# Two buffers for a group of W', the fifth transpose in another bank, and one chunk's stores on another queue

## The chip, the cores and the metric

The kernel runs on one core of a Trainium2 chip. The core's engines take their instructions in order, each from its own list, and wait for each other through semaphores: TensorE (PE in the profile; PEld is its loading of weights), VectorE (DVE), ScalarE (ACT), GpSimd (POOL) and SyncE (SP). SyncE only issues DMAs here; ScalarE issues some as well. The metric is the device time of one execution in microseconds (us), the median over several.

## The reference, cut to what matters

The output is a mix of two branches, weighted per token by a gate `g`. Branch A is a Fourier transform along the hidden and the sequence dimension, real part only. Branch B picks experts per head by two small score tables and sums their outputs.

```python
def reference(x, dft_seq_re, dft_seq_im, dft_hid_re, dft_hid_im, w_q, k1, k2, u, v, gate_w):
    g = sigmoid((x * gate_w).sum(-1, keepdims=True))
    # branch A
    a = einsum("bsd,ed->bse", x, dft_hid_re)
    b = einsum("bsd,ed->bse", x, dft_hid_im)
    y = einsum("ts,bse->bte", dft_seq_re, a) - einsum("ts,bse->bte", dft_seq_im, b)
    # branch B, per token and head: q = x w_q in two halves of 128
    s1, s2 = q1 @ k1.T, q2 @ k2.T              # 16 scores each
    # the best 2 of each, the best 2 of their 4 sums, softmax of those: gates; their pairs: experts
    out = sum over heads and picks of gates * gelu(x . u[expert]) * v[expert]
    return g * y + (1 - g) * out
```

Shapes: 2048 tokens, width 640, 32 heads, 16 x 16 = 256 experts, float32.

## The kernel before

All matrix products are done in float32 by a split: each operand is cut into a high and a low half (ScalarE writes the high half, line 122; GpSimd or VectorE subtracts it to get the low half, line 123), and three matmuls, high x high, high x low and low x high (`mm3`, lines 127 to 129), make one product.

The program is written in the order in which it is issued. It has 128 **pieces** of branch A (`seq_piece`): two matrices (real, imaginary), 4 chunks of 512 tokens, 16 pieces each. A piece is 15 matmuls of 128x512 into banks 0 to 4 and splits the matrix block of the piece three further on (`WS`, a ring of four). A block is loaded five pieces ahead (`wf`, line 159). A table `then`, filled by `at(n, ...)`, hangs other work behind piece n. At the end of a chunk ScalarE copies the five banks into the stage `ST` (line 220), VectorE multiplies the five parts with the gate (line 192, `gate_piece`), and the parts are stored to DRAM as `pd`, the partial sums P (line 201, `store_piece`).

In the first pieces the scores' weights are prepared: W', which is `w_q` multiplied with the keys. It is made in 8 groups G of 128 columns. For a group, a burst of 32 small matmuls (`w_part`, line 320) fills banks 5 and 6 in turn (`ps_s`), ScalarE copies both halves into the tile `wp` (line 325), and five transposes (`w_transposes`, line 331) turn the 640 rows around; ScalarE and VectorE write the result as a high and a low half into `WU` (lines 333 and 334). Four transposes are issued in one call, ahead of the next group's burst, the fifth a piece later in a second call. Both calls write into bank 7 (`ps_t`). The burst of group G is hung behind piece 6 + 3G; only behind piece 28 do two calls stand next to each other: the fifth transpose of group 6 and then the four of group 7. `wp` has one buffer. A copy into it therefore waits until the fifth transpose of the group before has been done, though that stands a piece later in TensorE's order.

From piece 31 on the scores, the picks and the experts' sums are put among the pieces. After the last piece comes a **last part** of 70 **steps** (`step`): the sequence product's second stage, written as sums of blocks, with operands loaded back from DRAM (`ra`). Step m uses the split operand m (in the tiles `WP` for m mod 6 below 2, else in `WS`), which was split five steps earlier (`split_step`), and 6 or 9 matmuls. The last chunk's stores (q = 7) are hung behind step 1 of it. `split_v` (a split of `v`, whose high half's and low half's parts ScalarE negates in line 736) and `split_z` (the operands `zo`, whose products VectorE makes in lines 851 and 852) fall into the same stretch.

DMAs take turns on eight semaphores, in the order in which the program issues them, whichever engine issues. A DMA waits until the one before it on its semaphore has landed; in the lists of instructions these are DMAHW0 to DMAHW7.

Of the kernel before, what the change touches and what calls it, by code (L numbers as in the profile page):

```python
# [8 lines left out]
F32 = mybir.dt.float32  # L9
# [7 lines left out]
P = 128  # L17
S = 2048
D = 640
# [8 lines left out]
NC = S // TC  # L28
# [62 lines left out]
def gated_mix_kernel(ctx: ExitStack, tc: tile.TileContext, xT, xn, dreT, dimT, wsre, wsim, wq, kT, uT, vv, gw, out):  # L91
    nc = tc.nc
# [9 lines left out]
    def rotate(what, n):  # L102
        turn[what] = (turn.get(what, -1) + 1) % n
        return turn[what]

    def bank(n, shape=(P, TC), dt=F32):
        return psum.tile(list(shape), dt, name=f"b{n}", tag=f"b{n}")

    def ps_s(shape=(P, TC)):
        return bank(5 + rotate("pss", 2), shape)  # L110

    def ps_t(shape, dt=F32):
        return bank(7, shape, dt)
# [17 lines left out]
    pd = {(w, c): dram.tile([KD, P, TC], F32, name=f"pd{w}{c}", tag=f"pd{w}{c}") for w in range(2) for c in range(NC)}  # L131
# [49 lines left out]
    grow, staged, P22 = {}, {}, {}  # L181
# [14 lines left out]
    def store_piece(q):  # L196
        w, c = divmod(q, NC)
        if q == NC + 1:
            P22.update((d, staged[q, d]) for d in range(KD))
        for d in range(KD):  # L200
            nc.scalar.dma_start(pd[w, c][d], staged.pop((q, d)))

    def seq_piece(n):
        w, c, s = pieces[n]
# [18 lines left out]
    for q in range(2 * NC):  # L223
        n = NT * (q + 1)
        at(n + (2 if q == 0 else -2 if q > 1 else -1), load_row, q)
        at(n + (7 if q == 0 else 0), gate_piece, q)
        at(n + (8 if q == 0 else 1), store_piece, q)
# [3 lines left out]
    p1 = p1_stack.enter_context(tc.tile_pool(name="p1", bufs=1, reuse_waits="tile"))  # L231
# [43 lines left out]
    t = ps_t([P, 512])  # L275
# [28 lines left out]
    wqs, wps, wp = {}, {}, {}  # L304
# [8 lines left out]
    def w_part(m):  # L313
        G, r, n = m // 4, m // 2 % 2, m % 2
        if r == 0:
            wps[G, n] = ps_s()
        ps = wps[G, n]
        w = wqs.pop(m)
        for j in range(4):
            nc.tensor.matmul(ps[32 * j:32 * j + 32, :HALF], kp[:, 8 * G // H, r, :], w[:, j], start=(r == 0),  # L320
                             stop=(r == 1))
        if r == 1:
            if n == 0:
                wp[G] = p1.tile([P, D], F32, name="wp", bufs=1)
            nc.scalar.activation(wp[G][:, n * HALF:(n + 1) * HALF], wps.pop((G, n))[:, :HALF], AF.Copy)

    def w_transposes(G, k0, k1):
        f = wp[G]
        t = ps_t([P, 4, P])
        for k in range(k0, k1):  # L330
            nc.tensor.transpose(t[:, k - k0, :], f[:, k * P:(k + 1) * P], identf)  # L331
        h = WH[:, k0:k1, P * G:P * (G + 1)]
        nc.scalar.activation(h, t[:, :k1 - k0], AF.Copy)  # L333
        nc.vector.tensor_sub(WL[:, k0:k1, P * G:P * (G + 1)], t[:, :k1 - k0], h.bitcast(F32))  # L334
# [35 lines left out]
    for G in range(NG + 1):  # L370
        b = 6 + 3 * G - 2 * (G == NG)
        if G:
            at(b, w_transposes, G - 1, 0, 4)
        if G < NG:
            for m in range(4 * G, 4 * G + 4):
                at(b, w_part, m)
            for i, m in enumerate(range(4 * G + WQB, 4 * G + WQB + 4)):
                at(b + i // 2, load_wq, m)
        if G:
            at(b + 1, w_transposes, G - 1, 4, KD)  # L380
# [702 lines left out]
```

## Time and profile before

| | |
|---|---|
| median of 3 runs | 782.41 us (782.23 to 783.89) |
| the profiled execution | 782.4 us |
| its span in the profile | 780.6 us |
| mean granted clock of TensorE | 0.998 of full speed |
| matmuls of branch A, W', scores, experts and last part | 4116 |
| DMA traffic | 130.32 MB, mean 167 GB/s |

The profile is one execution. Times are counted from the start of its span, which is a little shorter than the execution's own time, since what lies around the first and last instruction is not in it. A row of the timeline has the start, the duration, the engine, the line of the kernel, the operation, what is written and read, a count, and in brackets how long the engine had been idle and what ended that. ACTq and SPq rows are DMA issues of ScalarE and SyncE. Busy TensorE means that matmuls are in flight; a matmul's own duration of 0.39 us is longer than the 0.23 us after which the next one starts, since they overlap.

### The profile page before, as it was taken

The page shows a single profiled execution, that of the slowest core. Times are in us where ns is not written, and L with a number is a line of the kernel's source. Part 1 is how long each engine was busy: PE and PEld are TensorE (multiplying, and loading weights), DVE is VectorE, ACT ScalarE, POOL GpSimd, SP SyncE. Part 2 cuts the span into 40 slices and gives each one's busy share as a digit, 9 for nine tenths or more (in the row PEclk, how much of TensorE's full clock was granted, in tenths as well). Part 3 has the DMA queues.
Part 4 walks back from the last instruction along what each step waited for, and adds up shares of the span by engine and source line. Part 5 has one row for each costly group of instructions (what it writes and reads, how often), then busy time and mean ns, then how long its engine had stood idle before and what let it go on. Part 6 is the DMA issues. An engine that isn't in the chain of part 4 may idle for free.

```text
span 780.6 us, 11020 instructions
## 1 busy us (share of the span) xinstructions
PE 769.4 (99%) x4116; PEld 624.5 (80%) x4116; DVE 564.5 (72%) x660; ACT 274.0 (35%) x445; POOL 333.7 (43%) x233
## 2 busy tenths in 40 slices
PE   9999998999999999999999999999999999999997
PEld 6777776888888888888888888888888877888886
DVE  5742032279799799999989889698989857728561
ACT  5435223322233531533532461311324533424350
POOL 5432324323432324234156574343447463558270
PEclk9999999999999999999999999999999999999999
DMA  9887894512212241221353443558945767477321
GB/s 339 330 300 192 346 337 148 178 51 88 69 53 71 69 159 57 65 86 54 97 169 123 152 147 94 162 185 291 300 174 174 237 241 243 127 253 242 122 81 68
DMA packets 75509, 130.32 MB, mean 167 GB/s; under 512 B 17088, under 2 KB 24128, under 8 KB 75200
## 3 DMA queue, kind: packets, MB, share of 16 engines
q1 hardware_dynamic: 62704, 112.18, 43.4%
q10 hardware_dynamic: 12752, 17.45, 6.2%
q8 instruction: 32, 0.52, 0.3%
q14 instruction: 21, 0.17, 0.1%
HBM read 102.84 MB, written 25.17 MB: 164 GB/s over the span
## 4 chain that ended last, share of the span: by engine, by line
PE 88%; DVE 4%; issue 3%; POOL 3%; DMA 1%; ACT 0%; SPq 0%; DVEq 0%; POOLq 0%; ACTq 0%
PE b L127 28%; PE b L128 28%; PE b L129 28%; PE b L320 2%; POOL WS L123 1%; PE b L625 1%; POOL WP L123 1%; DMA wf<-in_wsre 1%; PE b L331 1%; DVE tf L710 1%; DVE tf L713 1%; DVE ts L123 0%; DVE tmp L611 0%; DVE tf L711 0%; DVE hot L604 0%
## 5 line engine op out<-in xcount | busy, mean ns | idle before, releaser
L123 POOL TENSOR_TENSOR WS<-wf,WS 128x512 fp32r<-128x512 f32 x127 | 191.5, 1513 | 263.3 <-ACT WS L122 263.3
L127 PE MATMUL b<-WS,X 128*128 128x512 f32 x635 | 250.9, 395 | 0.0
L128 PE MATMUL b<-WS,X 128*128 128x512 f32 x635 | 247.8, 390 | 0.2 <-POOL WS L123 0.2
L129 PE MATMUL b<-WS,X 128*128 128x512 f32 x635 | 247.6, 390 | 0.0
L127 PEld LDWEIGHTS b<-WS,X 128*128 128x128 f32 x635 | 119.4, 188 | 29.2 <-issue 4.1
L129 PEld LDWEIGHTS b<-WS,X 128*128 128x128 f32 x635 | 119.5, 188 | 25.2
L128 PEld LDWEIGHTS b<-WS,X 128*128 128x128 f32 x635 | 119.5, 188 | 24.8 <-POOL WS L123 0.8
L122 ACT ACTIVATE WS<-wf 128x512 fp32r<-128x512 f32 x128 | 80.7, 631 | 136.8 <-PE b L129 83.3
L123 POOL TENSOR_TENSOR xl<-xf,xh 128x640 fp32r<-128x640 f32 x16 | 27.1, 1694 | 84.6 <-ACT xh L122 84.6
L127 PE MATMUL b<-WU,xh 128*128 128x512 f32 x160 | 62.3, 390 | 0.0
L128 PE MATMUL b<-WU,xh 128*128 128x512 f32 x160 | 62.3, 390 | 0.0
L129 PE MATMUL b<-WU,xl 128*128 128x512 f32 x160 | 62.2, 389 | 0.0
L439 DVE TENSOR_REDUCE mm<-sc 128x64 f32<-128x1024 f32 x32 | 38.9, 1217 | 27.0 <-ACT sc L425 26.4
L123 POOL TENSOR_TENSOR WS<-ra,WS 128x512 fp32r<-128x512 f32 x32 | 44.9, 1423 | 31.2 <-ACT WS L122 22.4
L425 ACT ACTIVATE sc<-b 128x512 f32<-128x512 f32 x32 | 19.8, 619 | 108.0 <-PE b L129 102.3
L441 DVE TENSOR_TENSOR eq<-sc,mm 128x1024 f16<-128x1024 f32 x32 | 49.9, 1559 | 1.1
L611 DVE TENSOR_TENSOR tmp<-b,mask 128x512 f32<-128x512 f32 x32 | 22.0, 689 | 34.8 <-PE b L625 33.8
L334 DVE TENSOR_TENSOR WU<-b,WU 128x512 fp32r<-128x512 f32 (+1 forms) x16 | 7.8, 490 | 50.8 <-ACT WU L333 50.8
L123 POOL TENSOR_TENSOR WP<-ra,WP 128x512 fp32r<-128x512 f32 x18 | 27.7, 1546 | 33.5 <-ACT WP L122 33.4
L192 DVE SCALAR_TENSOR_TENSOR ST<-ST,grow 128x512 f32<-128x512 f32 x40 | 37.0, 987 | 4.1 <-ACT ST L220 4.1
L445 DVE TENSOR_REDUCE rr<-eq 128x64 f16<-128x1024 f16 x32 | 39.0, 1219 | 1.0
L122 ACT ACTIVATE WS<-ra 128x512 fp32r<-128x512 f32 x46 | 28.3, 630 | 28.0 <-PE b L129 16.7
(156 smaller groups left out, 1257.0 us busy)
## 6 DMA issues: line engine op xcount, KB each, us to landing
wq<-in_wq SPq DMA_DIRECT2D x32, 640.0 KB, 6.8
wf<-in_wsre SPq DMA_DIRECT2D x64, 256.0 KB, 4.8
wf<-in_wsim SPq DMA_DIRECT2D x64, 256.0 KB, 3.6
ra<-pd SPq DMA_DIRECT2D x50, 256.0 KB, 4.1
pd<-ST ACTq DMA_DIRECT2D x40, 256.0 KB, 3.1
xr<-in_xn SPq DMA_DIRECT2D x16, 320.0 KB, 5.8
xf<-in_xT SPq DMA_DIRECT2D x16, 320.0 KB, 3.3
ra<-pqs SPq DMA_DIRECT2D x20, 256.0 KB, 5.1
```

Of the source, the lines that this page charges most:

```text
L122: nc.scalar.activation(h, f, AF.Copy)
L123: eng.tensor_sub(l, f, h.bitcast(F32))
L127: nc.tensor.matmul(o, wh, ah, start=first, stop=False, skip_group_check=more)
L128: nc.tensor.matmul(o, wh, al, start=False, stop=False, skip_group_check=more)
L129: nc.tensor.matmul(o, wl, ah, start=False, stop=last, skip_group_check=more)
L192: nc.vector.scalar_tensor_tensor(f, f, -1.0 if w else 1.0, g, op0=OP.mult, op1=OP.mult)
L320: nc.tensor.matmul(ps[32 * j:32 * j + 32, :HALF], kp[:, 8 * G // H, r, :], w[:, j], start=(r == 0), stop=(r == 1))
L425: nc.scalar.activation(scs[i].rearrange("p h e -> p (h e)")[:, c], ps, AF.Copy)
L439: nc.vector.tensor_reduce(m, sc, op=OP.max, axis=AX.X)
L441: nc.vector.tensor_tensor(eq, sc, m[:, :, None].to_broadcast([P, HH, E]), op=OP.is_equal)
L445: nc.vector.tensor_reduce(r, eq, op=OP.max, axis=AX.X)
L611: nc.vector.tensor_tensor(tmp, t.rearrange("p m (e t) -> p (m e) t", t=4), mask4[:, None, :].to_broadcast([P, 8 * E, 4]), op=OP.mult)
```

## The change

Three edits: `wp` gets two buffers; the second call of the transposes (the fifth, `k0` = 4) takes its bank from `ps_s` (banks 5 and 6 in turn) instead of bank 7; and the five stores of the last chunk are issued by SyncE instead of ScalarE.

```diff
@@ store_piece
+        eng = nc.sync if q == 2 * NC - 1 else nc.scalar
         for d in range(KD):
-            nc.scalar.dma_start(pd[w, c][d], staged.pop((q, d)))
+            eng.dma_start(pd[w, c][d], staged.pop((q, d)))
@@ w_part
             if n == 0:
-                wp[G] = p1.tile([P, D], F32, name="wp", bufs=1)
+                wp[G] = p1.tile([P, D], F32, name="wp", bufs=2)
@@ w_transposes
         f = wp[G]
-        t = ps_t([P, 4, P])
+        t = ps_s((P, 4, P)) if k0 else ps_t([P, 4, P])
```

One line is added ahead of line 201, so lines behind it have a number higher by one in the changed kernel.

The first place is TensorE behind piece 28. The number behind a name is that of the tile; `b7_1140` is a tile in bank 7, `wp_999` and `wp_1106` are groups 6 and 7. Before:

```order
L129 MATMUL b4_699<-WS_88,X_442 128x512
L331 MATMUL b7_1140<-identf_148,wp_999 128x128 [waits DVE_49]
L331 MATMUL b7_1144<-identf_148,wp_1106 128x128 [waits DVE_49]
L331 MATMUL b7_1144<-identf_148,wp_1106 128x128
L331 MATMUL b7_1144<-identf_148,wp_1106 128x128 [waits Activation_49]
L331 MATMUL b7_1144<-identf_148,wp_1106 128x128
```

And now:

```order
L129 MATMUL b4_699<-WS_88,X_442 128x512
L332 MATMUL b5_1140<-identf_148,wp_999 128x128 [waits Activation_49]
L332 MATMUL b7_1144<-identf_148,wp_1106 128x128 [waits DVE_49]
L332 MATMUL b7_1144<-identf_148,wp_1106 128x128
L332 MATMUL b7_1144<-identf_148,wp_1106 128x128 [waits Activation_49]
L332 MATMUL b7_1144<-identf_148,wp_1106 128x128
```

The order is the same. The fifth transpose has moved to bank 5 and waits for ScalarE, which empties that bank of group 7's burst. The first of the four still waits for VectorE, but for the four of group 6, which were the last in bank 7.

The second place is ScalarE in the last part, at the last chunk's stores (`pd13` is that chunk of P). Before:

```order
L736 ACTIVATE ts_4959<-vxl_5322 128x256 [waits DVE_49]
L122 ACTIVATE WP_5185<-ra_5208 128x512 [waits DMAHW0_49,PE_49,Pool_49]
L201 DMA pd13_76<-ST_68 128x512 [waits DMAHW6_49]
L201 DMA pd13_76<-ST_68 128x512 [waits DMAHW0_49]
L201 DMA pd13_76<-ST_68 128x512 [waits DMAHW2_49]
L201 DMA pd13_76<-ST_68 128x512 [waits DMAHW4_49]
L201 DMA pd13_76<-ST_68 128x512 [waits DMAHW6_49]
L122 ACTIVATE WP_5185<-ra_5210 128x512 [waits DMAHW3_49,PE_49,Pool_49]
L122 ACTIVATE WS_88<-ra_5235 128x512 [waits DMAHW5_49,PE_49,Pool_49]
```

And now:

```order
L737 ACTIVATE ts_4959<-vxl_5322 128x256 [waits DVE_49]
L122 ACTIVATE WP_5185<-ra_5208 128x512 [waits DMAHW0_49,PE_49,Pool_49]
L122 ACTIVATE WP_5185<-ra_5210 128x512 [waits DMAHW3_49,PE_49,Pool_49]
L122 ACTIVATE WS_88<-ra_5235 128x512 [waits DMAHW5_49,PE_49,Pool_49]
L122 ACTIVATE zo_5374<-ra_5286 128x512 [waits DVE_49]
```

The splits of steps 6, 7 and 8 (`ra_5208`, `ra_5210`, `ra_5235`) now follow each other; before, the five stores stood between the first and the second.

The third place is SyncE's list in the same stretch, with the loads of the next operands (`pqs1`, `pqs2`). Now:

```order
L770 DMA ra_5327<-pqs1_77 128x512 [waits DMAHW2_49,PE_49]
L770 DMA ra_5327<-pqs1_77 128x512 [waits DMAHW3_49]
L202 DMA pd13_76<-ST_68 128x512 [waits DMAHW4_49,DVE_49]
L202 DMA pd13_76<-ST_68 128x512 [waits DMAHW5_49,DVE_49]
L202 DMA pd13_76<-ST_68 128x512 [waits DMAHW6_49,DVE_49]
L202 DMA pd13_76<-ST_68 128x512 [waits DMAHW7_49,DVE_49]
L202 DMA pd13_76<-ST_68 128x512 [waits DMAHW0_49,DVE_49]
L770 DMA ra_5346<-pqs1_77 128x512 [waits DMAHW1_49,DVE_49]
L770 DMA ra_5346<-pqs1_77 128x512 [waits DMAHW2_49]
L770 DMA ra_5091<-pqs2_78 128x512 [waits DMAHW3_49,Pool_49]
```

Before, the loads stand in the same order without the stores between them. The stores wait for VectorE's product with the gate, each for its own part, and the loads behind them wait for other semaphores than before.

## The prediction

> **What bounds the kernel now.** I read the busy times first, then who waited for whom on TensorE, then the granted clock in the stretches where it waited. Of the profile's first part, one line matters:
>
> ```profile
> PE 769.4 (99%) x4116; PEld 624.5 (80%) x4116; DVE 564.5 (72%) x660; ACT 274.0 (35%) x445; POOL 333.7 (43%) x233
> ```
>
> TensorE (PE) works for 769.4 of the 780.6 us of the span, so only about 11 us can be won without taking matmuls away. No edit here takes any away. The waits of PE over the whole span (us in total, times, longest) say where those 11 us lie, apart from the last stores:
>
> ```profile
> PE b L331 <- DVE WU L334: 3.5, 1, 3.5
> PE b L277 <- DVE warm L274: 1.2, 1, 1.2
> PE b L128 <- POOL WP L123: 0.8, 1, 0.8
> PE b L128 <- POOL WS L123: 0.8, 2, 0.6
> PE b L213 <- ACT WS L122: 0.4, 1, 0.4
> ```
>
> Two of them belong to the start. The other three places are one transpose (line 331) that waited 3.5 us for VectorE, and two matmuls of the last part that waited for GpSimd's low halves. I take the places in turn.
>
> **The transposes: what goes.** PE's rows (start, duration) around the long wait, with undisturbed neighbours, show how matmuls and transposes follow each other:
>
> ```profile
> 122.66 0.60 PE L331 MATMUL b<-identf,wp 128*128 128x128 f32 x4
> 123.19 2.36 PE L320 MATMUL b<-wq,kp 128*32 128x320 f32 x32
> ...
> 129.02 0.27 PE L331 MATMUL b<-identf,wp 128*128 128x128 f32 x1
> 132.77 1.11 PE L331 MATMUL b<-identf,wp 128*128 128x128 f32 x4 [3.48 <-DVE WU L334]
> 133.53 0.78 PE L127 MATMUL b<-WS,X 128*128 128x512 f32 x1
> ...
> 135.80 0.39 PE L129 MATMUL b<-WS,X 128*128 128x512 f32 x1
> ...
> 137.87 0.39 PE L129 MATMUL b<-WS,X 128*128 128x512 f32 x1
> ...
> 138.43 0.39 PE L128 MATMUL b<-WS,X 128*128 128x512 f32 x1
> ```
>
> At 129.02 the fifth transpose of group 6 goes into bank 7, and the four of group 7 stand right behind it in the same bank. They start at 132.77, when the fifth has been copied out. Only here do the two calls meet without a chunk's piece between them. The copying out is late because of what ScalarE and VectorE do from 129 on:
>
> ```profile
> 129.38 0.77 ACT L325 ACTIVATE wp<-b 128x320 f32<-128x320 f32 x2 [5.49 <-PE b L331]
> ...
> 132.11 0.27 ACT L333 ACTIVATE WU<-b 128x128 fp32r<-128x128 f32 x1
> ...
> 132.42 0.29 DVE L334 TENSOR_TENSOR WU<-b,WU 128x128 fp32r<-128x128 f32 x1 [1.51 <-ACT WU L333]
> ```
>
> ScalarE stood still for 5.49 us: its copies into `wp` for group 7 wait until the fifth transpose has read the only buffer. Behind them in its order come three splits, and only then the fifth's copy. With two buffers these copies need only the burst of line 320, which ends at 123.19 + 2.36 = 125.55, and are done by about 126.4. The three splits then run before 129, and the fifth's copy follows its transpose at once.
>
> The second edit makes the rest certain: the fifth transpose goes into a bank of the bursts, which ScalarE has emptied by 126.4. The four of group 7 use bank 7, last read by VectorE's subtraction for group 6, a whole piece earlier. So both calls find their banks free, and I cost their waits at nothing.
>
> The price of the wait is more than 3.48 us, as the granted clock (PEclk, the column behind the busy times) shows. These rows give, for a stretch, its length and the engines' busy time:
>
> ```profile
> 129.00:132.70 3.70, 0.29 (x2) 0.00 (x0) 0.71 (x2) 3.00 (x7) 1.55 (x2) 0.96 0.00 0
> 132.70:136.00 3.30, 3.23 (x10) 2.75 (x11) 1.19 (x3) 1.42 (x3) 3.30 (x3) 0.53 0.23 47
> ```
>
> After the wait PE ran at 0.53 of its clock until about 135.8, so four transposes took 1.11 us instead of 0.60. I therefore measure the gain at the sixth matmul behind them, where the pace is whole again, at 135.80. Undisturbed matmuls follow each other by 0.23 us (135.80 to 137.87 in nine). A fifth transpose between two of them adds 0.10 (138.43 less 137.87 less 2 x 0.23). Four transposes take 0.53 until the next starts (123.19 less 122.66). Without the wait the four start at 129.12, the first matmul at 129.65, and the sixth at 129.65 + 5 x 0.23 = 130.80. The gain is 135.80 less 130.80 = **5.0 us**: 3.65 of waiting and 1.35 of slow clock.
>
> In the other groups ScalarE waits for the fifth transpose in the same way, but that costs PE nothing now, since its waits above have no row for it; the end of those waits gains nothing. A group's second burst bank is now also read by VectorE for the fifth transpose, but ten microseconds before the next burst; I cost that at nothing too.
>
> **What is late next there.** The scalar and vector work shifts earlier with PE. One thing is tied to something else: SyncE's loads, which stand behind a load into `xf` whose buffer GpSimd reads.
>
> ```profile
> 131.15 3.03 POOL L123 TENSOR_TENSOR xl<-xf,xh 128x640 fp32r<-128x640 f32 x2 [8.13 <-ACT xh L122]
> 134.22 0.80 SPq L352 DMA_DIRECT2D xf<-in_xT  x2
> ```
>
> GpSimd waited 8.13 us for ScalarE's split, which is one of the three behind the `wp` copies. With those at 126.4 instead of 130.15 it starts some 3.8 us sooner, and so does the load. Against PE's 5.0 the pieces of `wf` behind it are 1.2 us later than now, and PE waits for none of them now. Later, a uniform shift needs an engine that follows PE and is not itself behind. Waits of VectorE from 145 to 620 us:
>
> ```profile
> DVE mm L439 <- ACT sc L425: 26.4, 5, 12.6
> DVE tmp L611 <- PE b L625: 20.2, 10, 3.4
> ```
>
> It stood idle for PE or for PE's results 15 times; so it follows, and the 5.0 us arrive whole.
>
> **The stores: what goes.** PE around its two late waits:
>
> ```profile
> 635.00 0.39 PE L129 MATMUL b<-WP,DD 128*128 128x512 f32 x1
> 635.46 0.50 PE L127 MATMUL b<-WP,DD 128*128 128x512 f32 x1
> 636.81 0.50 PE L128 MATMUL b<-WP,DD 128*128 128x512 f32 x1 [0.85 <-POOL WP L123]
> 637.15 0.39 PE L129 MATMUL b<-WP,DD 128*128 128x512 f32 x1
> ...
> 640.82 0.39 PE L127 MATMUL b<-WS,DD 128*128 128x512 f32 x1
> 641.82 0.50 PE L128 MATMUL b<-WS,DD 128*128 128x512 f32 x1 [0.61 <-POOL WS L123]
> ```
>
> These are steps 7 and 9. At its pace the third row of step 7 would stand at 635.00 + 3 x 0.23 = 635.69; it stands at 637.15, so the place costs 1.46. In step 9 the second matmul would start at 641.05 instead of 641.82, and restarting costs 0.11 (0.34 behind the wait instead of 0.23): 0.88. Both together are **2.34 us**, the most the third edit can give. Its cause is on ScalarE and GpSimd:
>
> ```profile
> 630.93 3.72 ACTq L201 DMA_DIRECT2D pd<-ST  x4
> 634.78 0.63 ACT L122 ACTIVATE WP<-ra 128x512 fp32r<-128x512 f32 x1 [3.39 <-DMA pd<-ST]
> ...
> 631.47 1.76 POOL L123 TENSOR_TENSOR WP<-ra,WP 128x512 fp32r<-128x512 f32 x1 [4.21 <-ACT WP L122]
> 635.49 1.27 POOL L123 TENSOR_TENSOR WP<-ra,WP 128x512 fp32r<-128x512 f32 x1 [2.25 <-ACT WP L122]
> 636.72 1.29 POOL L123 TENSOR_TENSOR WS<-ra,WS 128x512 fp32r<-128x512 f32 x1
> 637.96 2.57 POOL L123 TENSOR_TENSOR zo<-ra,zo 128x512 fp32r<-128x512 f32 x2
> ```
>
> Four stores held ScalarE for 3.72 us, so the split of step 7 came late and GpSimd stood still for 2.25. Without them ScalarE splits step 7 right behind step 6, and GpSimd goes on at 633.23 without a gap. How fast it goes on is the unknown. From 632.00 to 634.51 VectorE still has two products of the weights `z`, and the two engines delay each other:
>
> ```profile
> 623.83 3.43 POOL L123 TENSOR_TENSOR WS<-ra,WS 128x512 fp32r<-128x512 f32 x2
> ...
> 632.00 1.78 DVE L851 TENSOR_TENSOR ra<-ra 128x512 f32<-128x512 f32 x1
> 633.82 0.69 DVE L852 TENSOR_TENSOR ra<-ra 128x512 f32<-128x512 f32 x1
> ```
>
> GpSimd's subtraction took 1.72 beside busy VectorE (3.43 for two), 1.27 alone; the product took 1.78 against 0.69. Undelayed, GpSimd ends step 7 at 634.50, step 8 at 635.75, both `zo` at 638.25 and step 9 at 639.55. PE now wants step 9's low half at 641.05 less 1.46 = 639.59, so the whole 2.34 is won. With steps 7 and 8 at 1.72 each, step 7 ends at 634.95 (PE wants it at 635.46 to 635.69), step 8 at 636.67, `zo` at 639.2 and step 9 at 640.5: PE waits 0.9 and pays 0.11 for the restart, and 1.3 us are won. I take **1.3**, since both products are still to come when GpSimd would go on; 0 and 2.34 are the ends.
>
> [...]
>
> **What the stores do on SyncE.** Five issues and their waits now stand ahead of 18 loads. They wait for VectorE's products with the gate, done by 628.94. The first load behind them waited 8.8 us anyway:
>
> ```profile
> SPq L769 <- DVE ra L848: 8.8, 1, 8.8
> ...
> 639.98 1.15 ACT L122 ACTIVATE WP<-ra 128x512 fp32r<-128x512 f32 x2
> ```
>
> It was let go near 630.45, after VectorE's split of `v`, which comes behind those products. So the stores issue in a hole of SyncE's and delay no load; they leave earlier than now. ScalarE wants that load only at 639.98.
>
> **The sum.** The profiled execution took 782.4 us, its span 780.6 and 1.8 around it; the median of the runs is 782.41, so no correction is needed. 782.4 - 5.0 - 1.3 = **776.1 us**.
>
> **Rivals.** *The stores win nothing*: GpSimd stays late in the last part, because VectorE's products hold it or the loads come later on SyncE. For it: GpSimd is back to back from 635.49 to step 9. Against it: the 2.25 us gap in it goes. Time 782.4 - 5.0 = 777.4, give or take 0.3.
>
> *Part of the long wait stays*: the four transposes of group 7 wait for `wp`, whose copies now come just ahead of them, or PE meets a later split. For it: GpSimd and ScalarE still have three splits between. Against it: 126.4 against 129.12 leaves 2.7 us. With between 0.3 and 3.5 us left at PE the time is 777.7 to 780.8. [...]
>
> *The first two edits do not do what they say*: bank 7 stays the meeting point. Then only the stores count, 782.4 - 1.3 = 781.1, no measurable change. The rows of the two calls, with different banks, speak against it.
>
> *Slower, through SyncE*: the stores hold the queue and the loads behind them starve the last part. A load takes SyncE about 5 us to land, so from 630.45 it is there at 635.5, and ScalarE wants it at 639.98: 4.5 us are free. To eat the 6.3 us won elsewhere the stores would have to hold SyncE for about 11 us past 630.45, though what they wait for is done at 628.94. Time above 784 from there on.
>
> **How the numbers follow.** Forecast, 774.8 to 777.1: 0.66. Stores win nothing, 777.1 to 777.7: 0.17. Part of the wait stays, 777.7 to 780.8: 0.10. No effect, within 0.2% (780.8 to 784.0, about what a measurement of this kernel can tell from no change): 0.04. Slower: 0.03. The low end is the whole 7.3 us, 775.1, with 0.3 of spread; the high end takes in the second case: 774.8 to 777.7 holds 0.83. Faster by over 0.2%: 0.66 + 0.17 + 0.10 = 0.93.
>
> **What would show it.** Right: no wait of line 332 on VectorE, ScalarE's `wp` copies near 126, and a clock of 1.00 from 129 to 136. In the last part, ScalarE's split of step 7 right behind that of step 6, GpSimd without a gap from 631 less 5, and one wait of PE under 1 us at step 9. Wrong: a new wait of PE between 129 and 150, a slow clock without a wait, or SyncE's loads of the last part later against PE than now.

## The result and the profile after

The changed kernel takes 775.41 us (median of 6 runs, 774.75 to 775.75) beside 783.15 us (median of 6, 782.23 to 784.94): a ratio of 0.9899, 95% interval 0.9885 to 0.9912. The profiled executions are 775.65 and 782.4 us, 6.75 us apart. The forecast was 776.1, with 774.8 to 777.7 around it.

TensorE in the first part of the page, then the waits of PE over the whole span (us in total, times, longest):

```profile
PE 767.0 (99%) x4116; PEld 623.2 (81%) x4116; DVE 565.7 (73%) x660; ACT 275.2 (36%) x445; POOL 332.6 (43%) x233
```

```profile
PE b L128 <- POOL WS L123: 1.3, 2, 0.8
PE b L278 <- DVE warm L275: 1.2, 1, 1.2
PE b L214 <- ACT WS L122: 0.2, 1, 0.2
```

The transposes' row is gone, and so is that of step 7 (`WP`). What is left on GpSimd is one wait of the start and one of 0.75 us at step 9. PE at the place of the long wait (start, duration):

```profile
129.18 0.71 PE L332 MATMUL b<-identf,wp 128*128 128x128 f32 x5
129.64 0.48 PE L127 MATMUL b<-WS,X 128*128 128x512 f32 x1
...
130.88 0.40 PE L129 MATMUL b<-WS,X 128*128 128x512 f32 x1
```

The five transposes now run as one group, and the sixth matmul behind them starts at 130.88 instead of 135.80. The same stretches as before, with the granted clock behind the busy times, show it at full speed:

```profile
129.00:132.70 3.70, 3.70 (x20) 3.08 (x19) 1.59 (x3) 1.70 (x4) 3.70 (x3) 1.00 0.37 107
132.70:136.00 3.30, 3.30 (x16) 2.69 (x15) 0.29 (x1) 0.80 (x2) 1.96 (x3) 1.00 1.00 349
```

ScalarE and GpSimd there, and SyncE's load that stood behind GpSimd:

```profile
125.24 0.98 ACT L326 ACTIVATE wp<-b 128x320 f32<-128x320 f32 x2 [1.19 <-PE b L321]
...
129.48 0.28 ACT L334 ACTIVATE WU<-b 128x128 fp32r<-128x128 f32 x1 [1.19 <-PE b L332]
...
127.22 3.10 POOL L123 TENSOR_TENSOR xl<-xf,xh 128x640 fp32r<-128x640 f32 x2 [5.39 <-ACT xh L122]
...
130.34 0.80 SPq L353 DMA_DIRECT2D xf<-in_xT  x2
```

The copies into `wp` are released by the burst (line 321) and no longer by the fifth transpose; the fifth's own copy comes 0.3 us behind it. The last part, on ScalarE, GpSimd, PE and SyncE:

```profile
625.84 1.14 ACT L122 ACTIVATE WP<-ra 128x512 fp32r<-128x512 f32 x2
...
626.53 3.48 POOL L123 TENSOR_TENSOR WP<-ra,WP 128x512 fp32r<-128x512 f32 x2 [4.21 <-ACT WP L122]
629.97 1.75 POOL L123 TENSOR_TENSOR WS<-ra,WS 128x512 fp32r<-128x512 f32 x1
...
635.51 0.50 PE L128 MATMUL b<-WS,DD 128*128 128x512 f32 x1 [0.75 <-POOL WS L123]
...
619.50 4.92 SPq L202 DMA_DIRECT2D pd<-ST  x5
625.50 11.55 SPq L770 DMA_DIRECT2D ra<-pqs  x18
```

Steps 6 and 7 are split back to back on both engines. GpSimd takes 1.74 us for each and 1.75 for step 8. SyncE issues the five stores as VectorE's products come and is done a microsecond before the 18 loads may start.

Where the 6.7 us of the span come from can be read by comparing the same instructions in both traces. Up to the fifth transpose (129.02 before, 129.18 now) the changed kernel is 0.16 us behind, as its start was. At the sixth matmul it is 4.92 ahead, so the place gave about 5.1. The bursts of the experts' sums stand 4.95 us ahead from the first (437.24 before, 432.29 now) to the one at 619.02 (614.07 now), and 6.35 ahead behind step 9 (644.58 and 638.23): the last part gave 1.40. The remaining 0.4 or so lie behind the last matmul, where the last stores land, and no edit touches them.

### The profile page after: what moved, and what is told of

Its sections match the earlier page's. It is cut to its first block, busy times and chain, and to the rows that moved or that the text cites. A ratio compares the mean times of both kernels' runs of the same rounds, so it can differ in the third digit from the quotient of the medians.

```text
span 773.9 us, 11025 instructions
## 1 busy us (share of the span) xinstructions
PE 767.0 (99%) x4116; PEld 623.2 (81%) x4116; DVE 565.7 (73%) x660; ACT 275.2 (36%) x445; POOL 332.6 (43%) x233
## 4 chain that ended last, share of the span: by engine, by line
PE 89%; DVE 4%; issue 3%; POOL 2%; DMA 1%; SPq 0%; DVEq 0%; ACT 0%; POOLq 0%
PE b L127 29%; PE b L128 28%; PE b L129 28%; PE b L321 2%; POOL WS L123 1%; PE b L626 1%; DMA wf<-in_wsre 1%; DMA ra<-pqs 1%; DVE tf L711 1%; PE b L332 1%; POOL WP L123 1%; DVE tf L714 1%; DVE ts L123 0%; DVE tmp L612 0%; DVE tf L712 0%
## 5 line engine op out<-in xcount | busy, mean ns | idle before, releaser
L192 DVE SCALAR_TENSOR_TENSOR ST<-ST,grow 128x512 f32<-128x512 f32 x40 | 35.1, 938 | 4.1 <-ACT ST L221 4.1
```

The costliest lines, as they stand in the source:

```text
L192: nc.vector.scalar_tensor_tensor(f, f, -1.0 if w else 1.0, g, op0=OP.mult, op1=OP.mult)
```

## The experiments

The executions of the kernel before lie between 780.7 and 785.1 us in all that follows. Each comparison has the kernel before on the same chip; the first four kernels share one set of it (median 782.36).

**One edit alone: two buffers.**

```diff
-                wp[G] = p1.tile([P, D], F32, name="wp", bufs=1)
+                wp[G] = p1.tile([P, D], F32, name="wp", bufs=2)
```

> Only the second buffer of wp; the fifth transpose stays in bank 7. Theory: the long wait was a late copying out, not the shared bank alone. ScalarE reaches the fifth's copy (0.28 us) at once and VectorE (0.29 us) follows, so the four of group 7 still wait, but only about 0.9 us, and the granted clock from 132 to 136 us stays 1.00. Time 4.1 us below the kernel before. Rival (bank 7 is the whole cause): the wait stays near 3.5 us and nothing is won. Rival (any wait here halves the clock): 0.9 us of wait and 1.35 of slow clock stay, 2.8 us won.

Measured: 778.02 us (777.76 to 778.67), ratio 0.9947 (0.9934 to 0.9960), 4.3 us below. The row of PE's wait and the granted clock behind it:

```profile
PE b L331 <- DVE WU L334: 0.7, 1, 0.7
```

```profile
132.70:136.00 3.30, 3.30 (x16) 2.68 (x15) 0.29 (x1) 0.80 (x2) 1.69 (x2) 1.00 0.99 341
```

The bank is still shared, and the wait is 0.7 us long instead of 3.5: its length was the late copying out. Both rivals fall: the wait did not stay, and the clock behind the short one is whole.

**One buffer, but no shared bank.** The second edit cannot stand alone: with one buffer the fifth transpose would wait for a burst bank whose copy waits for the fifth transpose. So the four transposes of the last group were moved instead.

```diff
-        t = ps_t([P, 4, P])
+        t = ps_s((P, 4, P)) if k0 == 0 and G == NG - 1 else ps_t([P, 4, P])
```

> One buffer of wp; the four transposes of group 7 go into a burst bank, so that they do not meet the fifth of group 6 in bank 7. Theory: they now wait for the copies into wp, which still wait for the fifth (ScalarE idle about 34 us in 7 waits, as before): about 1.1 us of wait at PE, no slow clock, 3.9 us below the kernel before. Rival (the shared bank is the whole cause): no wait of PE, 5.1 us won.

Measured: 778.16 us (777.57 to 778.39), ratio 0.9946 (0.9933 to 0.9959), 4.2 us below, with a wait of 0.6 us where the theory had 1.1; the rival, no wait, falls. What ended PE's wait has changed, and ScalarE's old wait is still there (tile `wp`: what its engine waited for):

```profile
PE b L331 <- ACT wp L325: 0.6, 1, 0.6
```

```profile
  PE b L331: 34.1, 7
```

So the 3.5 us needed both: the one buffer that made ScalarE late and the bank that made PE wait for ScalarE's lateness. Either remedy alone, the second buffer or another bank for these transposes, takes out most of it, and the two edits together (777.36 us, below) 0.7 to 0.8 us more than one.

**The stores alone.**

```diff
+        eng = nc.sync if q == 2 * NC - 1 else nc.scalar
         for d in range(KD):
-            nc.scalar.dma_start(pd[w, c][d], staged.pop((q, d)))
+            eng.dma_start(pd[w, c][d], staged.pop((q, d)))
```

> Only the last chunk's stores on SyncE. Theory: the 3.5 us wait and the slow clock stay; step 7 waits no more, step 9 about 0.75 us; 1.4 us below the kernel before. Rival (the last part's gain needs the earlier edits, or the stores are not its cause): no difference, 0 +- 0.3 us.

Measured: 780.85 us (778.84 to 782.30, 12 runs), ratio 0.9978 (0.9967 to 0.9988), 1.5 us below. More of its executions than of the kernel before kept a whole clock (a mean of 0.999 or more: 5 of 12 against 2 of 17), so compare like with like: 1.3 us between the medians of those with a lowered clock (781.05 and 782.39), 1.8 of those without (779.10 and 780.87). Step 7 has no wait left. Its profiled execution, the fastest of the twelve, brought a surprise: the long wait is there, and the clock behind it is not lowered.

```profile
PE b L332 <- DVE WU L335: 3.5, 1, 3.5
```

```profile
132.70:136.00 3.30, 3.30 (x17) 2.76 (x16) 1.65 (x2) 1.42 (x3) 3.30 (x3) 1.00 0.35 111
```

**The first two edits without the stores.**

> Both edits of the transposes, the stores left on ScalarE. Theory: no wait of PE on a transpose, clock 1.00, and the waits of 0.85 and 0.61 us at steps 7 and 9 as before: 5.1 us below the kernel before. Rival (part of the 5.1 is lost later without the third edit): under 4 us won, with larger waits in the last part.

Measured: 777.36 us (776.74 to 778.05), ratio 0.9937 (0.9924 to 0.9950), 5.0 us below, with PE's wait of 0.9 us at step 7 still there. 5.0 and 1.5 make 6.5; the whole change, run again (next), is 7.3 below its own set of the kernel before, whose executions scatter. The parts add up within that scatter; the intervals of the ratios allow it.

**The whole change again, and three variants of the last part** (one chip; kernel before 782.9).

> The changed kernel again, beside the three next ones on one chip. Theory: the first two edits gave 5.0 us and the third 1.5 us apart, and they do not meet; so 6.5 to 7.0 us below the kernel before, every execution within about 1 us, none with a mean clock below 0.999.

Measured: 775.58 us (775.21 to 775.65), ratio 0.9908 (0.9895 to 0.9922). No mean clock was below 0.999.

Next the stores were left on ScalarE but hung later; they then write what the stage holds after step 4's copies, so that chunk of P has other values.

```diff
-    at(n + (8 if q == 0 else 1), store_piece, q)
+    at(n + (8 if q == 0 else 8 if q == 2 * NC - 1 else 1), store_piece, q)
```

> Both edits of the transposes; the last chunk's stores stay on ScalarE but are hung behind step 8 instead of step 1. Theory: what the third edit won is ScalarE's place in the list, not the queue of SyncE; step 7's split runs at once, and the time is that of the changed kernel within 0.4 us, if the stage's buffers, which the copies of steps 4 and 9 write, are not the next wait. Rival (those copies now wait behind nothing, but the copy after step 4 needs the stored part and stands ahead of the stores): ScalarE's copy order changes and a new wait takes 1 us or more.

Measured: 777.69 us (776.78 to 779.26), ratio 0.9938 (0.9926 to 0.9951): no better than with the stores left where they were. Half of the theory is in the rows: step 7's split follows step 6's at once, from 625.60 on, and PE has no wait at step 7. Its condition fails. The late stores hold ScalarE for 4.47 us, and then its copy into the stage's fifth buffer (line 959) waits 4.00 us for a store to land, since the store still has to read that buffer; PE waits for the copy:

```profile
634.19 4.47 ACTq L201 DMA_DIRECT2D pd<-ST  x4
638.78 0.63 ACT L122 ACTIVATE WS<-ra 128x512 fp32r<-128x512 f32 x1 [4.24 <-DMA pd<-ST]
```

```profile
643.42 0.60 ACT L959 ACTIVATE ST<-b 128x512 f32<-128x512 f32 x1 [4.00 <-DMA pd<-ST]
...
644.07 0.50 PE L127 MATMUL b<-WS,DD 128*128 128x512 f32 x1 [0.66 <-ACT ST L959]
```

That wait and its restart cost about 0.9 us; the profiled execution is 1.2 above the whole change's and the median 2.1, and the rest is not explained. So the stores cost something at both places tried on ScalarE, but for different reasons, and this run does not settle whether the engine that issues or the place in its list is what counts. An earlier place on ScalarE is untested. In the kernel before it stands idle just ahead of the stores' place, for longer than the 4.92 us in which SyncE issues all five in the changed kernel:

```profile
630.45 0.42 ACT L736 ACTIVATE ts<-vxl 128x256 fp32r<-128x256 f32 x1 [5.60 <-DVE vxl L123]
```

Then VectorE's products for the first `zo` were left out.

```diff
-            nc.vector.tensor_tensor(a, a, f, op=OP.mult)
-            nc.vector.tensor_tensor(a, a, g, op=OP.mult)
+            if b or n:
+                nc.vector.tensor_tensor(a, a, f, op=OP.mult)
+                nc.vector.tensor_tensor(a, a, g, op=OP.mult)
```

> The changed kernel without VectorE's four products of the first operands zo (they hold the activations alone, so the experts' part of one chunk is wrong). Theory: the remaining wait at step 9 (0.75 us, 0.86 with the restart) comes from VectorE and GpSimd delaying each other; GpSimd's subtractions of steps 7 and 8 take 1.27 instead of 1.75 us, and PE has no wait there: 0.9 us below the changed kernel. Rival (GpSimd simply has too much in a row, seven subtractions): step 9 still waits 0.3 us or more.

Measured: 774.6 us (774.22 to 774.77), ratio 0.9896 (0.9882 to 0.9909), 1.0 below the whole change. GpSimd's rows for steps 6, 7 and 8:

```profile
626.61 2.55 POOL L123 TENSOR_TENSOR WP<-ra,WP 128x512 fp32r<-128x512 f32 x2 [4.21 <-ACT WP L122]
629.12 1.29 POOL L123 TENSOR_TENSOR WS<-ra,WS 128x512 fp32r<-128x512 f32 x1
```

Two take 2.55 us instead of 3.48, the third 1.29 instead of 1.75, and PE has no wait in the last part. The wait at step 9 came from VectorE and GpSimd hindering each other.

Last, a version that should be faster: VectorE, idle from 630.6, subtracts step 9's low half.

```diff
-            split(raw[key], *sp[m], nc.vector if what in ("s2", "s3") else nc.gpsimd)
+            split(raw[key], *sp[m], nc.vector if what in ("s2", "s3") or m == 9 else nc.gpsimd)
```

> The changed kernel with the low half of step 9 subtracted by VectorE, which is idle then. Theory: the wait at step 9 goes, and step 10 on GpSimd is early by one subtraction: 0.9 us below the changed kernel. Rival (VectorE's subtraction waits for ScalarE's split, which stands behind both zo copies, and PE waits for VectorE instead): less than 0.3 us.

Measured: 774.69 us (774.19 to 774.76), ratio 0.9896 (0.9880 to 0.9911), 0.9 below the whole change, all four executions below all four of it. PE's only waits are those of the start:

```profile
PE b L278 <- DVE warm L275: 1.2, 1, 1.2
PE b L128 <- POOL WS L123: 0.5, 1, 0.5
PE b L214 <- ACT WS L122: 0.4, 1, 0.4
```

**The clock behind a wait.** The unlowered clock of the third experiment asked when a wait lowers it. Four more runs change the wait's length. First shorter, by hanging ScalarE's two splits of the score operand a piece later, and longer, by two copies more:

```diff
     for a in range(2):
-        at(n - 3, split_xT, 0, a)
+        at(n - 2, split_xT, 0, a)
```

```diff
         at(n - 3, split_xT, 0, a)
+    at(n - 3, lambda: [nc.scalar.activation(p1.tile([P, D], F32, name="idle", bufs=1), xf[0][:, 0].rearrange("p k c -> p (k c)"), AF.Copy) for a in range(2)])
```

> The kernel before, but ScalarE's two splits of the score operand (1.36 us) are hung one piece later, out of the long wait. Theory: PE's wait shrinks from 3.5 to about 2.1 us, and a wait that short never halves the clock, so executions lie within about 1 us and none has a mean clock below 0.999; 1.4 us below the fast-clock executions of the kernel before (780.9), so near 779.5. Rival (any wait of this kind can halve the clock): the spread of 3 to 4 us and mean clocks of 0.995 to 0.998 stay, median near 781.

> The kernel before with two more copies of 640 columns (about 1.36 us, into a tile that nothing reads) on ScalarE inside the long wait. Theory: PE's wait grows to about 4.85 us, and now every execution has the halved clock behind it for some us: no mean clock of 0.999 or more, median 1.4 us and the missing fast-clock executions above the kernel before, 784 to 786. Rival (the halving is by chance and not by the wait's length): median 1.4 us above with about as many fast-clock executions as before (2 or 3 in 17).

Measured: 781.22 us (780.37 to 781.73) for the short one, ratio 0.9978 (0.9968 to 0.9987), and 784.55 (783.96 to 785.12) for the long one, ratio 1.0024 (1.0014 to 1.0033). The short wait with its clock behind it, and then the long one with two of its stretches:

```profile
PE b L331 <- DVE WU L334: 2.2, 1, 2.2
```

```profile
132.70:136.00 3.30, 3.30 (x9) 2.62 (x8) 1.02 (x2) 2.63 (x5) 1.80 (x3) 0.50 0.00 0
```

```profile
PE b L331 <- DVE WU L334: 4.9, 1, 4.9
```

```profile
135.00:140.00 5.00, 5.00 (x13) 3.88 (x13) 1.02 (x2) 1.42 (x3) 1.55 (x2) 0.51 0.96 328
140.00:141.00 1.00, 1.00 (x6) 0.82 (x5) 0.00 (x0) 0.00 (x0) 0.00 (x0) 1.00 0.82 311
```

Theory for the short wait falls: 2.2 us of idle lowered the clock to 0.50 for 3.4 us, and five of nine executions have a mean clock of 0.996 or 0.997. For the long wait it holds: none of nine is above 0.998, and the clock stays halved until about 140, 6.8 us. Next a wait between 0.7 and 2.2 (added to the kernel with two buffers), and the short one again for another profile:

```diff
+        if k0 and G == NG - 2:
+            for a in range(3):
+                nc.scalar.activation(p1.tile([P, P], F32, name="idle", bufs=1), t[:, 0], AF.Copy)
```

> The kernel with two buffers of wp alone (0.69 us of wait, 778.0 us), and three more copies of the fifth transpose's 128 columns on ScalarE ahead of the real one (into a tile that nothing reads), so a wait of about 1.5 us. Theory after the runs with 0.69, 2.2, 3.5 and 4.9 us: the clock is set from a window in which PE did too little, and 1.5 us idle in it is not too little; every execution at a mean clock of 0.999 or more, 0.8 us above the kernel with two buffers, 778.8. Rival (any wait from about 1 us on can do it): some executions at 0.996 to 0.998, with a spread above 1.5 us.

> The kernel with the 2.2 us wait again, for another profile: of its nine executions four had a mean clock of 1.00 and five 0.996 or 0.997, with hardly any difference in time. Theory: if this profile has the clock of 1.00 between 132 and 137 us, the way from the fifth transpose to the first score takes 16.8 us (14.3 of the changed kernel and 2.4 of wait), against 18.35 in the profile with the halved clock. Rival (the mean clock of an execution misses the halving): 18 us or more beside a clock of 1.00.

Measured: 779.03 us (778.61 to 780.20), ratio 0.9962 (0.9949 to 0.9975), with 1.5 us of wait, all six executions at 0.999 or 1.000; the theory holds for the clock, though the spread of 1.6 us is the rival's, and what the executions at 779.7 and 780.2 lost is not known. The short wait gave 780.94 us (780.01 to 781.42), ratio 0.9979 (0.9967 to 0.9991), four of eight at 1.00, and this profile is one of them:

```profile
132.70:136.00 3.30, 3.30 (x17) 2.67 (x16) 1.02 (x2) 2.55 (x5) 1.81 (x2) 1.00 0.00 0
```

```profile
142.53 0.63 ACT L122 ACTIVATE WS<-wf 128x512 fp32r<-128x512 f32 x1 [5.61 <-DMA wf<-in_wsre]
...
143.70 0.50 PE L127 MATMUL b<-WS,X 128*128 128x512 f32 x1 [0.76 <-ACT ST L220]
```

From the fifth transpose (129.39) to the first score's matmul (147.25) it takes 17.86 us, neither 16.8 nor quite 18.35. The rival that the record misses a halving falls, for the matmuls did run at full pace. PE instead came to the chunk's end too early and waited there for ScalarE's copies of the banks. These stood behind a split that waited 5.61 us for the load of a matrix block: with the moved splits GpSimd's `xl` starts at 134.19 instead of 131.15, SyncE's load into `xf` leaves at 137.31 instead of 134.22, and the loads of `wf` stand behind it. In the profile with the halved clock the same split waited until 142.67, and the slower PE had no wait there. That is why this kernel gains little from a full clock.

**Where the clock's windows lie.** The profiles tell more than the executions' mean clocks. Six of the fourteen are read here: the kernel before, the changed kernel, the stores alone, the two of the short wait and the long wait. Where the clock changes more than once in one of them, the times lie a whole number of 3.413 us apart: in the kernel before it falls at 132.37 and is back at 135.78, and for the first short wait it falls at 132.69, is back at 136.10 and falls again behind the last matmul at 777.81, which is 188 times 3.413 behind 136.10. That last fall is also in profiles whose clock stayed whole until then (772.77 in the changed kernel, 775.59 with the stores alone, 779.14 in the second profile of the short wait), so windows of 3.41 us can be counted back from it there. By these windows, with TensorE's busy time as the second number and the clock behind the busy times: the kernel before, the first short wait, the stores alone, the second short wait, and the long wait from its second window on.

```profile
128.96:132.37 3.41, 0.33 (x2) 0.00 (x0) 0.43 (x1) 2.98 (x7) 1.22 (x1) 1.00 0.00 0
132.37:135.78 3.41, 3.01 (x9) 2.57 (x10) 1.47 (x3) 1.44 (x4) 3.41 (x4) 0.50 0.18 26
```

```profile
129.27:132.69 3.42, 1.19 (x8) 0.80 (x7) 0.72 (x2) 1.78 (x6) 1.20 (x1) 1.00 0.00 0
132.69:136.10 3.41, 3.41 (x9) 2.62 (x8) 1.02 (x2) 2.64 (x5) 1.91 (x3) 0.50 0.00 0
```

```profile
127.06:130.47 3.41, 1.82 (x9) 1.23 (x7) 0.39 (x1) 1.50 (x4) 0.00 (x0) 1.00 0.00 0
130.47:133.88 3.41, 1.52 (x9) 1.35 (x10) 0.52 (x3) 2.34 (x7) 3.13 (x3) 1.00 0.00 0
133.88:137.30 3.42, 3.42 (x17) 2.79 (x16) 1.75 (x3) 1.29 (x4) 2.60 (x2) 1.00 0.75 214
```

```profile
127.19:130.60 3.41, 2.47 (x12) 1.76 (x10) 0.00 (x0) 0.84 (x3) 0.00 (x0) 1.00 0.00 0
130.60:134.02 3.42, 2.13 (x12) 1.83 (x13) 1.53 (x4) 2.35 (x7) 1.27 (x1) 1.00 0.00 0
```

```profile
133.12:136.54 3.42, 2.54 (x8) 2.24 (x9) 1.05 (x3) 1.89 (x5) 2.13 (x2) 0.50 0.42 141
136.54:139.95 3.41, 3.41 (x9) 2.64 (x8) 0.27 (x1) 0.04 (x1) 1.29 (x1) 0.50 0.97 335
```

So in these profiles a wait counted by how much of it fell into one window. The short wait put 2.23 us of idle into one window and lowered the clock of the next; split into 0.94 and 1.29 it did not, and neither did the 3.5 us of the third experiment, split into 1.59 and 1.89. In the six profiles every window at a whole clock around the wait and behind the last matmul with up to 1.89 us of idle was followed by a whole clock and every one with 2.23 us or more by half of it (behind the last matmul 1.32 us in the kernel before kept the clock of the next window, 2.94 in the changed kernel halved it). The other eight profiles have mean clocks of 0.999 or 1.000, and the longest wait read in them is 1.5 us. The windows lie differently in each profile against the wait; that this also decides between the executions without a profile is an inference, though their shares fit it. A wait of 1.5 us can't put that much into one window (none of six executions was lowered), and one of 4.9 us puts over 2.4 into one wherever the windows lie (all nine were). No window with an idle time between 1.89 and 2.23 was seen. Little was seen of the way back: at half clock 0.4 us of idle in a window (the kernel before) was followed by a whole clock, 0.9 (the long wait) by half of it again.

## Why the prediction was right

**The bound.** PE works for 99% of the span in both profiles, and nothing but its waits had to be counted. The runs bear that out: the time saved is waits of PE that are gone or shorter, and the lowered clock behind one of them.

**The transposes: 5.0 forecast, 5.1 in the profiles.** The step that ScalarE's `wp` copies would come near 126 and the fifth's copy at once is in the rows (125.24 to 126.22, and 129.48). The two parts of the sum are not of one kind, though. The waiting, 3.65 us, is in both profiles that keep it (the kernel before and the stores alone). The 1.35 us of slow clock were taken from one execution as if they were fixed, and they are not: of the 59 executions of the kernel before in the four comparisons, six have a mean clock of 1.00, and all six lie between 780.7 and 781.1; the others lie from 781.9 to 785.1. Against the six the first two edits win about 3.4 us (777.36), against the median 5.0. It was luck that the profiled execution was one near the median. The two parts forecast 6.3 us together; the profiles have 6.75 between them and the medians 7.7, because the kernel before, run beside the changed one, had a median of 783.15 and not the 782.4 that the sum starts from. With the wait the scatter went as well: over 4 us before (780.7 to 785.1), 1.0 after.

**What is late next: nothing, as forecast.** GpSimd's `xl` starts 3.9 us sooner (127.22 instead of 131.15; 3.8 forecast), SyncE's load 3.9, and PE has no wait between 129 and 619: the bursts stay ahead by 4.95 throughout.

**The stores: 1.3 forecast, 1.40 in the profiles.** Step 7 has no wait. GpSimd's subtractions of steps 7 and 8 took 1.74 and 1.75 us against the 1.72 taken for them, and step 9 waits 0.75 instead of 0.9. That this rest is VectorE's doing was only argued and is now shown by the kernel without products, where step 9 has no wait and GpSimd takes 1.27 us for each of steps 6 and 7 and 1.29 for step 8: with VectorE's products beside them steps 6 and 7 took 0.47 us longer each (1.74 less 1.27).

**The stores on SyncE: hidden, as forecast.** SyncE's first load behind them leaves at 625.50, which is 630.45 less the 4.95 by which all is earlier.

**The rival on part of the wait** did not come: PE has no wait left there. What a shorter or a longer wait does to the clock the runs show: 2.2 us lowered it in 9 of 17 executions (mean clock below 0.999), 3.5 us did not in 6 of 59 of the kernel before and 5 of 12 with the stores alone, and 0.7 and 1.5 us never did, in 11 (of five with 0.6 us, in the second experiment, one has 0.998, which is not explained). A window did not have to be idle throughout: 1.19 us of work in one of 3.42 us, in the first short wait, did not keep the clock of the next.

## What to carry to other kernels

A single buffer whose reader stands later in another engine's order holds back everything behind the copy into it, far from the place where the wait is counted (here ScalarE stood still for 5.49 us, and PE then for 3.48); look at what the releasing engine had queued, not only at the releaser. Issue stores from an engine that has nothing urgent behind them: here four of them held ScalarE for 3.72 us ahead of a split, and at the later place tried the wait came back at the buffer that the late store still had to read (4.00 us of ScalarE's, 0.66 of PE's). Where a wait of TensorE is some 2 us or longer, do not take its clock penalty from one profile (2.2 us lowered the clock in 9 of 17 executions here): compare several executions' times and mean clocks, and see in the profile how the wait lies to the clock's windows.

## What was not expected of the hardware

TensorE's granted clock fell (to 0.50 in the profiles) behind waits of 2.2 us in about half of the executions, behind 3.5 us in nine of ten in the kernel before and seven of twelve with the stores alone, and behind 4.9 us in all nine; never behind 0.7 or 1.5 us. In the profiles where it fell behind a wait it stayed low for one window of 3.41 us, and for two behind the longest wait, and what decided in the six profiles read by windows was the idle time within one window: 1.89 us and less left the clock alone, 2.23 and more halved it. Most of the kernel before's scatter goes with it: its 59 executions lie from 780.7 to 781.1 at a mean clock of 1.000, from 781.9 to 782.9 at 0.996 to 0.998, and from 782.7 to 785.1 at 0.995; the 2.4 us within the last group are not explained. Two executions fit none of this: one with the stores hung later (0.996, 779.26 us) and one of the second experiment (0.998, 778.29 us), both of kernels whose profiles have no wait above 0.9 us but that of the start; their cause is open.
